# Two key pieces per output half, five shared relus, a later first y, and a mixed last-but-one tile

## Chip, cores and metric

One core of one Trainium2 chip. The metric is the device time of one execution in microseconds (us). The kernel before takes 1197.23 us (median of 3 runs, 1196.8 to 1197.61). Ratios further down are computed as the mean time of one kernel's runs over the mean of the other's runs of the same rounds, with a 95% interval; so they are not quite the ratio of the medians quoted beside them. A profiled execution has its own "span", which leaves out some 2 us of start and end.

## The reference

```python
def _attn_ref(u, v, z):                     # u, v: 8 x 3008 x 256; z: 8 x 3008 x 64
    scores = (1.0 / S) * np.matmul(z, z.transpose(0, 2, 1))
    attn = np.maximum(scores, 0.0) ** 2     # relu, then square
    return u * np.matmul(attn, v)

def _moe_ref(x, w_in, w_out):               # 24064 tokens, 256 -> 2048 -> 256
    h = x @ w_in
    return (h * np.cos(h)) @ w_out          # g = h cos(h); y = g w_out
```

The output is `_moe_ref` of `_attn_ref`, 24064 x 256 in fp32.

## The kernel before

The engines are named as in the profile: PE is TensorE (matmuls), ACT is ScalarE, DVE is VectorE, POOL is GpSimd, and SP issues the DMA of the turned pieces. SBUF is the working memory on the chip; PSUM is the memory that TensorE writes its sums to, divided into banks; a score group fills two of them, with 512 fp32 each in a partition. The 24064 tokens are 48 tiles, called columns while attention is computed for them: 8 batches of 6 columns, most of 512 tokens. For a column TensorE computes score groups (two key blocks of 128 keys each, against the column's 512 queries), ACT takes the relu out of PSUM, DVE squares it into a buffer A in SBUF, and TensorE multiplies A with v into two output halves, each gathered in two PSUM banks that are added at the end. The scores are symmetric, so many A pieces are not computed but turned (transposed) by DMA. A key piece is four key blocks of A, the unit in which the values are multiplied. There are three double banks E0, E1, E2 for scores, h and one output half, and two single banks M0, M1 for the other half and for y.

```python
    def emit_score(later=None):             # one score group
        ...
        e = E[take_e()]                     # a double bank: two halves of 512 fp32
        for t in range(2):
            nc.tensor.matmul(e[:, t, 0:Wt], zT[...], zT[...], ...)
        r = rpool.tile([P, 2, CW], FP16, name="r")
        nc.scalar.activation(r[:, :, 0:W], e[:, :, 0:W], AF.Relu)           # ACT
        def square():
            nc.vector.tensor_tensor(a4, r4, r4, ALU.mult)                   # DVE
        ...

    def gate_sum(s, b0, b1):                # the two banks of an output half, added
        sm = spool.tile([P, CW], FP32, name="sm")
        nc.scalar.copy(sm[:, 0:W], b0[:, 0:W])                              # ACT
        nc.vector.tensor_tensor(sm[:, 0:W], b1[:, 0:W], sm[:, 0:W], ALU.add)  # DVE
        return sm

    def phase_a_first(s, n, extra={}):      # columns 0, 1 and 2, one after the other
        pair = [E[ea][:, 0, :], E[ea][:, 1, :]]
        acc = [pair, M] if s == 1 else [M, pair]    # banks of output half 0 and half 1
        steps = [(dh, k) for I in range(NC) for dh in range(2)
                 for k in range(4 * I, min(4 * I + 4, last))] + [(2, last)]
        ...                                 # values, with the next column's scores between
        late_sums.extend(gate_sum(s, *acc[dh]) for dh in range(2))
        hold(late_sums[0][0:1, 0:1])        # POOL waits here, then loads u and (s = 1) w_out
        load_u(s + 1)
        e_order.append(ea)
```

The MoE stage s computes the h of tile s - 1 in 8 units (TensorE, into an E bank; ACT makes cos, DVE g) and the y of tile s - 2 between them. Stage 2 is the first one: it has the h of tiles 0 and 1, and the y of tile 0 between those. From tile 1 on, y is "mixed": Strassen-Winograd, seven products of half size in place of eight, with sums s1 on POOL and s2, s4 on DVE. The last two tiles (46, 47) are not mixed.

```python
    def mixed(m):
        return 1 <= m < NSLOT - 2           # NSLOT = 48
    order_y = (5, 1, 6, 7, 2, 3, 4)         # product 5 reads s1, 6 reads s2, 3 reads s4
    ...
        if n > 8:                           # stage 2, 16 h units: y block i stands behind
            after = (1, 3, 5, 7, 9, 11, 13, 14)     # h unit after[i], counted from 0
    ...
    phase_a_first(0, 12, {4: lambda: turn_late(4), 8: lambda: turn_late(5)})
    phase_a_first(1, 12)
    nc.gpsimd.dma_start(w_out16, moe_w_out.rearrange("(k p) f -> p k f", p=P))
    phase_a_first(2, 14)
```

Of the kernel before, what the change touches and what calls it, by code (L numbers as in the profile page):

```python
# [14 lines left out]
def kernel(  # L15
# [9 lines left out]
    nc = tc.nc  # L25
    AF = mybir.ActivationFunctionType
# [5 lines left out]
    P = 128  # L32
# [146 lines left out]
    turn_slots = {}  # L179
    done_groups = [0]  # L180

    def emit_score(later=None):
        b, J, I, h = groups[done_groups[0]]
        done_groups[0] += 1
        cut = I == J and not (b == 0 and J < 3)
        W = 2 * P if cut and h == 0 else width(J)
        zT = zTs[b]
        e = E[take_e()]
        for t in range(2):
            k = 4 * I + 2 * h + t  # L190
            half = t if h == 0 else 1 - t
            rows = slice(half * H, (half + 1) * H)
            Wt = min(W, (2 * h + t + 1) * P) if cut else W
            nc.tensor.matmul(  # L194
                e[:, t, 0:Wt],
                zT[rows, k * P:(k + 1) * P],
                zT[rows, J * CW:J * CW + Wt],
                start=True,
                stop=True,
            )  # L200
        key = (b, J, I)
        a = new_piece(key) if h == 0 else piece(key)
        r = rpool.tile([P, 2, CW], FP16, name="r")
        nc.scalar.activation(r[:, :, 0:W], e[:, :, 0:W], AF.Relu)  # L204
        def square():
            if I > J:
                a4 = a.rearrange("p (k t j) -> p t k j", k=4, j=P)[:, 2 * h:2 * h + 2, :, :]
                r4 = r.rearrange("p t (k j) -> p t k j", j=P)
                nc.vector.tensor_tensor(a4, r4, r4, ALU.mult)  # L209
            else:  # L210
                a4 = a.rearrange("p (k w) -> p k w", w=CW)[:, 2 * h:2 * h + 2, 0:W]
                nc.vector.tensor_tensor(a4, r[:, :, 0:W], r[:, :, 0:W], ALU.mult)  # L212

        if later is None:
            square()
        else:
            later.append(square)
        if h == 0:
            return
        if cut or (I > J and (b, J, I) not in direct):  # L220
            turns.append(((b, I), key))
            turns.sort(key=lambda t: t[0])
            turn_slots[key] = pieces[key]
            pending[pieces[key]] = "held"
# [122 lines left out]
    def phase_a_first(s, n, extra={}):  # L347
        b, J = s // NC, s % NC
        ea = e_order.pop(0)
        pair = [E[ea][:, 0, :], E[ea][:, 1, :]]  # L350
        acc = [pair, M] if s == 1 else [M, pair]
        last = NB - 1
        steps = [
            (dh, k)
            for I in range(NC)
            for dh in range(2)
            for k in range(4 * I, min(4 * I + 4, last))
        ] + [(2, last)]
        lo, hi = 5 if s == 0 else 2, 42
        at = {}  # L360
        for i in range(n):
            p = lo + (hi - lo) * i // (n - 1)
            at[p] = at.get(p, 0) + 1
        for i, (dh, k) in enumerate(steps):
            if i in extra:
                extra[i]()
            if dh == 2:
                emit_value(b, J, last, 0, 0, acc[0][0], False, True)
                emit_value(b, J, last, 1, 1, acc[1][1], False, True)
            else:  # L370
                for t in range(2):
                    emit_value(
                        b, J, k, t, dh, acc[dh][t], k == 0, k == last - 1 and t != dh
                    )
            if dh > 0 and (k % 4 == 3):
                drop_piece((b, J, k // 4))
                if s > 0:
                    emit_turns((0, 0), 1)
                    if k < 4:
                        turn_u(s)  # L380
                    elif k < 8:
                        for d in range(2):
                            gate_mul(s - 1, d, late_sums.pop(0))
            for _ in range(at.get(i, 0)):
                emit_score(later=squares if s == 0 and i == lo else None)
        if s == 0:
            turn_u(0)
        late_sums.extend(gate_sum(s, *acc[dh]) for dh in range(2))
        hold(late_sums[0][0:1, 0:1])
        load_u(s + 1)  # L390
        e_order.append(ea)
# [24 lines left out]
        )  # L416

    def mixed(m):
        return 1 <= m < NSLOT - 2

    F = NFT // 2
    T = 2 * P
# [38 lines left out]
            )  # L461
        nc.scalar.activation(y_outs[m][0][:, 1, :], acc, AF.Copy, bias=0.0, scale=inv_s2)

    def product(m, n):
        g = gs[m]
        nk, up, low = halves_of(m)
        nk = nk // P
        t = lambda i: w_mix[:, i, :, :]
        left, right = {
            1: (g[:, 0:F, up], w_out16[:, 0:F, 0:P]),  # L470
            2: (g[:, F:, up], w_out16[:, F:, 0:P]),
            3: (s4, w_out16[:, F:, P:D]),
            4: (g[:, F:, low], t(3)),
            5: (s1, t(0)),
            6: (s2, t(1)),
            7: (g[:, 0:F, low], t(2)),
        }[n]
        at = order_y.index(n) + (nk == 1 and n in order_y[4:])
        acc = M[at % 2][:, 0:nk * P]
        for ft in range(F):  # L480
            for k in range(nk):
                nc.tensor.matmul(  # L482
                    acc[:, k * P:(k + 1) * P],
                    left[:, ft, k * P:(k + 1) * P],
                    right[:, ft, :],
                    start=(ft == 0 and k == 0),
                    stop=(ft == F - 1 and k == nk - 1),
                )
        acc = acc.rearrange("p (k d) -> p k d", d=P)
        if n == 5:  # L490
            y_outs[m] = [opool.tile([P, 2, D], FP32, name="o") for i in range(2)]
            y_parts[m] = {}
        c11, c12, c21, c22 = (y_outs[m][i][:, 0:nk, d * P:(d + 1) * P] for i in range(2) for d in range(2))
        parts = y_parts[m]
        add = lambda dst, other: nc.vector.scalar_tensor_tensor(
            dst, acc, inv_s2, other, ALU.mult, ALU.add
        )
        if n in (1, 5, 6):
            parts[n] = ypool.tile([P, 2, P], FP32, name=f"p{n}")[:, 0:nk, :]
        if n in (1, 5):  # L500
            nc.scalar.activation(parts[n], acc, AF.Copy, bias=0.0, scale=inv_s2)
        elif n == 6:
            add(parts[6], parts[1])
            nc.gpsimd.tensor_tensor(c12, parts[6], parts[5], ALU.add)
        elif n == 7:
            add(c21, parts[6])
            nc.gpsimd.tensor_tensor(c22, c21, parts[5], ALU.add)
        elif n == 2:
            add(c11, parts[1])
        elif n == 3:  # L510
            add(c12, c12)
            store_half(m, 0, y_outs[m][0])
        else:
            add(c21, c21)
            store_half(m, 1, y_outs[m][1])

    def y_bank(m, k):
        if m == NSLOT - 1 and k == 3:
            return E[0][:, 0, 0:D]
        return M[k // 2][:, (k % 2) * D:(k % 2 + 1) * D]  # L520

    def y_block(m, ft, k):
        final = m == NSLOT - 1
# [58 lines left out]
    def phase_b(s):  # L582
        y, hs = s - 2, [(s - 1, i) for i in (0, 4, 1, 5, 2, 6, 3, 7)]
        if s == 2:
            hs = [(0, i) for i in range(8)] + hs
        for dh in range(len(late_sums)):
            gate_mul(s, 2 - len(late_sums), late_sums.pop(0), nc.gpsimd)
        if mixed(y):
            ys = [lambda n=n: product(y, n) for n in order_y]
            if mwidth(y) < CW:  # L590
                ys.insert(4, lambda: middle(y))
        else:
            ys = [lambda i=i: emit_y(y, i) for i in range(8)]
            ys[7] = lambda f=ys[7]: (f(), store_y(y))
        n = len(hs)
        if n > 8:
            after = (1, 3, 5, 7, 9, 11, 13, 14)
        elif mixed(y):
            after = (0, 1, 2, 3, 4, 5, 6, 6)
        else:  # L600
            after = (0, 1, 2, 3, 4, 5, 6, 6)
        for i, (m, unit) in enumerate(hs):
            times_c = emit_h(m, unit)
            if not mixed(y):
                times_c()
            for f, place in zip(ys, after):
                if place == i:
                    f()
            if mixed(y):
                times_c()  # L610
            if mixed(m) and unit >= 4:
                mix_early(m, unit - 4)
            if i in (1, 3, 5):
                emit_turns((0, 0), 1)
# [52 lines left out]
    emit_score(later=squares)  # L667
    emit_score(later=squares)
    turn_on_pe(2)
    copy_turned(2)  # L670
    squares.pop(0)()
    squares.pop(0)()
    M = [ppool.tile([P, CW], FP32, name=f"M{i}", tag=f"M{i}") for i in range(2)]

# [94 lines left out]
```

## Time and profile before

| | before |
|---|---|
| time, median | 1197.23 us |
| span of the profiled execution, clock | 1194.3 us, 1.0 |
| TensorE busy | 99% of the span |
| TensorE stands still near 24 us (column 0 to 1) | about 0.6 us |
| near 37 us (column 1 to 2) | 2.1 us |
| near 54 us (first y of the first MoE stage) | 1.7 us |
| anywhere behind that | never over 0.21 us |

How the lines are read: in the timeline a row has start, length, engine, source line, operation, tiles and shape, the number of instructions, and in brackets the idle time ahead and what ended it. A matmul's end is modelled; so a stop is best taken from start to start, against the usual pitch. The rows themselves are in the prediction.

### The profile page before, as it was taken

Reading aid. Unit: us, or ns where it says so; the run is one execution under the profiler, and the core shown is the slowest. Engines: PE = TensorE matmul, PEld = TensorE weight load, DVE = VectorE, ACT = ScalarE, POOL = GpSimd, SP = SyncE. Lnnn points to the kernel's source line nnn. Section 1 sums busy time; section 2 is a strip of 40 time slices with the busy share of each in tenths; the row PEclk is TensorE's granted clock in tenths of the full one; section 3 lists DMA queues with packets and bytes.
Section 4 is the critical chain, followed back from the end, with each engine's and each line's share of the span. In section 5 each row is a group of like instructions: output and inputs, shape, how many; then the busy total and the mean of one; then the engine's idle time right before and its main releaser. Section 6 shows DMA issues by size and latency. Waiting matters only on the chain.

```text
span 1194.3 us, 28924 instructions
## 1 busy us (share of the span) xinstructions
PE 1184.6 (99%) x11839; PEld 727.2 (61%) x11839; DVE 1008.6 (84%) x1293; ACT 795.1 (67%) x927; POOL 678.4 (57%) x707
## 2 busy tenths in 40 slices
PE   9899999999999999999999999999999999999998
PEld 4556655665566656566556665666656666665566
DVE  6798988888988898888988889888888888888775
ACT  7866666666766676666766676766766666666454
POOL 3186745557565573665647556476565765545450
PEclk9999999999999999999999999999999999999999
DMA  9999898769995699956999459974798838954301
GB/s 159 172 165 163 121 153 127 118 107 137 139 139 104 114 140 157 128 92 113 150 147 132 91 107 156 169 117 77 121 160 154 122 70 122 183 105 89 65 19 54
DMA packets 479861, 147.98 MB, mean 124 GB/s; under 512 B 404208, under 2 KB 479472, under 8 KB 479728
## 3 DMA queue, kind: packets, MB, share of 16 engines
q1 hardware_dynamic: 380752, 112.93, 54.5%
q0 software_dynamic: 97440, 32.78, 28.1%
q8 instruction: 92, 1.51, 0.5%
q10 hardware_dynamic: 1536, 0.43, 0.2%
q14 instruction: 41, 0.34, 0.1%
HBM read 66.32 MB, written 24.64 MB: 76 GB/s over the span
## 4 chain that ended last, share of the span: by engine, by line
PE 97%; ACT 1%; DVE 1%; issue 1%; ACTq 0%; DVEq 0%
PE E L403 27%; PE M L482 23%; PE M L258 20%; PE E L258 19%; PE E L194 5%; PE M L524 2%; ACT r L204 1%; PE M L459 1%; PE E L654 0%; DVE sm L270 0%; PE E L524 0%; DVE A L209 0%; DVE x L286 0%; DVE g L414 0%; PE M L677 0%
## 5 line engine op out<-in xcount | busy, mean ns | idle before, releaser
L411 ACT ACTIVATE c<-E 128x1024 f16<-128x1024 f32 (+1 forms) x384 | 385.6, 1006 | 218.0 <-PE E L403 214.8
L414 DVE SCALAR_TENSOR_TENSOR g<-E,c 128x1024 f16<-128x1024 f32 (+1 forms) x384 | 458.9, 1197 | 66.7 <-ACT c L411 65.7
L204 ACT ACTIVATE r<-E 128x512 f16<-128x512 f32 (+1 forms) x342 | 327.8, 967 | 114.1 <-PE E L194 108.4
L258 PEld LDWEIGHTS <-v 64*128 64x128 f16 x4512 | 246.8, 94 | 232.4 <-issue 20.6
L403 PE MATMUL E<-x,w_in 128*128 128x512 f16 (+1 forms) x1408 | 353.8, 375 | 0.0
L432 POOL TENSOR_TENSOR s<-g 128x512 f16<-128x512 f16 (+1 forms) x180 | 202.9, 1127 | 185.4 <-DVE g L414 138.9
L258 PE MATMUL M<-A,v 64*128 64x512 f16 (+1 forms) x2256 | 284.9, 372 | 2.1 <-ACT sm L269 1.2
L258 PE MATMUL E<-A,v 64*128 64x512 f16 (+1 forms) x2256 | 279.4, 372 | 0.0
L433 POOL TENSOR_TENSOR g<-g 128x512 f16<-128x512 f16 (+1 forms) x180 | 214.2, 1190 | 14.1
L403 PEld LDWEIGHTS <-w_in 128*128 128x128 f16 x1536 | 133.4, 98 | 108.6 <-issue 19.1
L482 PEld LDWEIGHTS <-g 128*128 128x128 f16 x2752 | 168.6, 98 | 39.8
L209 DVE TENSOR_TENSOR A<-r 128x1024 f16<-128x1024 f16 x240 | 173.3, 734 | 15.1 <-ACT r L204 14.3
L286 POOL TENSOR_TENSOR x<-sm,uT 128x512 f16<-128x512 f32 (+1 forms) x43 | 48.5, 1130 | 214.1 <-DVE sm L270 213.9
L482 PEld LDWEIGHTS <-s 128*128 128x128 f16 x2064 | 126.6, 98 | 30.6
L194 PE MATMUL E<-zT 64*128 64x512 f16 (+4 forms) x684 | 130.0, 356 | 0.5 <-ACT zT L647 0.3
L439 DVE TENSOR_TENSOR s<-s,g 128x1024 f16<-128x1024 f16 (+1 forms) x90 | 98.5, 1094 | 2.1 <-POOL s L432 2.1
L482 PE MATMUL M<-w_out,g 128*128 128x128 f16 x1376 | 91.5, 219 | 0.0
L482 PE MATMUL M<-w_mix,g 128*128 128x128 f16 x1376 | 91.5, 219 | 0.0
L482 PE MATMUL M<-w_mix,s 128*128 128x128 f16 x1376 | 91.5, 219 | 0.0
L212 DVE TENSOR_TENSOR A<-r 128x512 f16<-128x512 f16 (+1 forms) x102 | 80.7, 792 | 10.2 <-ACT r L204 9.4
L194 PEld LDWEIGHTS <-zT 64*128 64x128 f16 x684 | 39.3, 94 | 36.7 <-issue 2.2
L441 DVE TENSOR_TENSOR s<-g,s 128x1024 f16<-128x1024 f16 (+1 forms) x90 | 59.4, 662 | 0.0
(58 smaller groups left out, 657.6 us busy)
## 6 DMA issues: line engine op xcount, KB each, us to landing
out_dram<-o SPq DMA_DIRECT2D x87, 256.0 KB, 2.2
v<-in_v_dram POOLq DMA_DIRECT2D x40, 256.0 KB, 9.2
u<-in_u_dram POOLq DMA_DIRECT2D x40, 256.0 KB, 4.8
A<-A SPq DMA_TRANSPOSE x252, 5.2
z<-in_z_dram POOLq DMA_DIRECT2D x14, 192.0 KB, 10.6
z<-in_z_dram POOLq DMA_DIRECT2D x14, 176.0 KB, 6.3
v<-in_v_dram POOLq DMA_DIRECT2D x8, 192.0 KB, 12.0
u<-in_u_dram POOLq DMA_DIRECT2D x8, 192.0 KB, 4.0
```

The costliest lines, as they stand in the source:

```text
L194: nc.tensor.matmul(e[:, t, 0:Wt], zT[rows, k * P:(k + 1) * P], zT[rows, J * CW:J * CW + Wt], start=True, stop=True,)
L204: nc.scalar.activation(r[:, :, 0:W], e[:, :, 0:W], AF.Relu)
L209: nc.vector.tensor_tensor(a4, r4, r4, ALU.mult)
L212: nc.vector.tensor_tensor(a4, r[:, :, 0:W], r[:, :, 0:W], ALU.mult)
L258: nc.tensor.matmul(bank[:, 0:width(J)], vs[b, k // 4][t * H:(t + 1) * H, k % 4, dh * P:(dh + 1) * P], value_rhs(b, J, k, t), start=start, ...
L403: nc.tensor.matmul(e[:, f, 0:W], w_in16[:, k, ft * P:(ft + 1) * P], x[:, k, 0:W], start=(k == 0), stop=(k == 1),)
L411: nc.scalar.activation(c[:, :, 0:W], e[:, :, 0:W], AF.Sin, bias=half_pi, scale=inv_s2)
L414: return lambda: nc.vector.scalar_tensor_tensor(gs[m][:, 2 * i:2 * i + 2, 0:W], e[:, :, 0:W], 1.0, c[:, :, 0:W], ALU.mult, ALU.mult)
L432: nc.gpsimd.tensor_tensor(s1[:, f, 0:n], g[:, f, low], g[:, lower, low], ALU.add)
L433: nc.gpsimd.tensor_tensor(g[:, f, low], g[:, f, up], g[:, f, low], ALU.subtract)
L439: nc.vector.tensor_tensor(s2[:, f, 0:n], s1[:, f, 0:n], g[:, f, up], ALU.subtract)
L482: nc.tensor.matmul(acc[:, k * P:(k + 1) * P], left[:, ft, k * P:(k + 1) * P], right[:, ft, :], start=(ft == 0 and k == 0), stop=(ft == F - ...
```

## The change

The intent, as its words say: relieve ACT at the ends of the first columns (five relus shared with DVE), use the M banks later in columns 1 and 2 (two key pieces, that is eight key blocks, per output half), put the first y of stage 2 behind the third h unit, and take one matmul product in eight out of tile 46. The numbers in `shared_groups` count the score groups from 0, as the prediction does; the tables further down count them from 1. The diff, cut to its core:

```diff
+    shared_groups = {0, 14, 15, 26, 27}
 ...
-        nc.scalar.activation(r[:, :, 0:W], e[:, :, 0:W], AF.Relu)
+        n = 1 if shared else 2
+        nc.scalar.activation(r[:, 0:n, 0:W], e[:, 0:n, 0:W], AF.Relu)
+        if shared:
+            nc.vector.tensor_scalar(r[:, 1, 0:W], e[:, 1, 0:W], 0.0, None, ALU.max)
 ...
+            parts = [slice(0, 1), slice(1, 2)] if done == 0 else [slice(0, 2)]
+            for t in parts:
+                nc.vector.tensor_tensor(a4[:, t], r4[:, t], r4[:, t], ALU.mult)
 ...
+        run = 1 if s == 0 else 2
         steps = [
-            for I in range(NC)
+            for I in range(0, NC, run)
             for dh in range(2)
-            for k in range(4 * I, min(4 * I + 4, last))
+            for k in range(4 * I, min(4 * (I + run), last))
 ...
-        return 1 <= m < NSLOT - 2
+        return 1 <= m < NSLOT - 1
 ...
+        bank = 1 - k // 2 if m == NSLOT - 1 else k // 2          # y banks of the last tile
 ...
+                for i, n in enumerate((1, 5) + order_y[2:] if late else order_y)   # late: s == NSLOT
 ...
-            after = (1, 3, 5, 7, 9, 11, 13, 14)
+            after = (2, 4, 6, 7, 9, 11, 13, 14)
+        elif s == NSLOT:
+            after = (0, 1, 3, 4, 5, 6, 7)
 ...
+            if s == NSLOT and i in (1, 3):
+                for c in range(2):
+                    mix_late(y, "s2" if i == 1 else "s4", c)
 ...                                       # first group: its square ahead of a copy
+    squares.pop(0)()
     copy_turned(2)
-    squares.pop(0)()
```

More of the change, by code (lines that the diff above doesn't have):

```diff
@@ L180 @@
     done_groups = [0]
+    shared_groups = {0, 14, 15, 26, 27}
     def emit_score(later=None):
-        b, J, I, h = groups[done_groups[0]]
+        done = done_groups[0]
+        b, J, I, h = groups[done]
         done_groups[0] += 1
@@ L203, in emit_score @@
         r = rpool.tile([P, 2, CW], FP16, name="r")
-        nc.scalar.activation(r[:, :, 0:W], e[:, :, 0:W], AF.Relu)
+        shared = done in shared_groups
+        n = 1 if shared else 2
+        nc.scalar.activation(r[:, 0:n, 0:W], e[:, 0:n, 0:W], AF.Relu)
+        if shared:
+            nc.vector.tensor_scalar(r[:, 1, 0:W], e[:, 1, 0:W], 0.0, None, ALU.max)
         def square():
@@ L208, in square @@
                 r4 = r.rearrange("p t (k j) -> p t k j", j=P)
-                nc.vector.tensor_tensor(a4, r4, r4, ALU.mult)
             else:
                 a4 = a.rearrange("p (k w) -> p k w", w=CW)[:, 2 * h:2 * h + 2, 0:W]
-                nc.vector.tensor_tensor(a4, r[:, :, 0:W], r[:, :, 0:W], ALU.mult)
+                r4 = r[:, :, 0:W]
+            parts = [slice(0, 1), slice(1, 2)] if done == 0 else [slice(0, 2)]
+            for t in parts:
+                nc.vector.tensor_tensor(a4[:, t], r4[:, t], r4[:, t], ALU.mult)
         if later is None:
@@ L462, in middle, with product @@
         nc.scalar.activation(y_outs[m][0][:, 1, :], acc, AF.Copy, bias=0.0, scale=inv_s2)
-    def product(m, n):
+    def product(m, n, place):
         g = gs[m]
@@ L477, in product @@
         }[n]
-        at = order_y.index(n) + (nk == 1 and n in order_y[4:])
-        acc = M[at % 2][:, 0:nk * P]
+        acc = M[(place + (nk == 1 and place >= 4)) % 2][:, 0:nk * P]
         for ft in range(F):
@@ L489, in product @@
         acc = acc.rearrange("p (k d) -> p k d", d=P)
-        if n == 5:
+        if m not in y_outs:
             y_outs[m] = [opool.tile([P, 2, D], FP32, name="o") for i in range(2)]
@@ L519, in y_bank @@
             return E[0][:, 0, 0:D]
-        return M[k // 2][:, (k % 2) * D:(k % 2 + 1) * D]
+        bank = 1 - k // 2 if m == NSLOT - 1 else k // 2
+        return M[bank][:, (k % 2) * D:(k % 2 + 1) * D]
     def y_block(m, ft, k):
@@ L588, in phase_b @@
         if mixed(y):
-            ys = [lambda n=n: product(y, n) for n in order_y]
+            late = s == NSLOT
+            ys = [
+                lambda n=n, i=i: product(y, n, i)
+                for i, n in enumerate((1, 5) + order_y[2:] if late else order_y)
+            ]
             if mwidth(y) < CW:
```

## The prediction

> **What bounds the kernel now.** I read the page first, then the chain of waits, then the timeline of the first 80 us and of the last 80, and last the groups kept apart by form, for durations. From the page:
>
> ```profile
> PE 1184.6 (99%) x11839; PEld 727.2 (61%) x11839; DVE 1008.6 (84%) x1293; ACT 795.1 (67%) x927; POOL 678.4 (57%) x707
> PE 97%; ACT 1%; DVE 1%; issue 1%; ACTq 0%; DVEq 0%
> ```
>
> TensorE is busy 99% of the span and owns 97% of the chain that ended last. So the time is the sum of TensorE's work and of its few stalls; another engine matters only where TensorE stands still for it. The timeline shows where that is, all of it in the first columns and the MoE stage after them (figures: start us, length us; in brackets the idle time before and what ended it):
>
> ```profile
> 24.47 0.59 PE L258 MATMUL M<-A,v 64*128 64x512 f16 x3 [0.28 <-DVE sm L270]
> ...
> 37.69 0.37 PE L258 MATMUL M<-A,v 64*128 64x512 f16 x1 [1.22 <-ACT sm L269]
> 38.65 0.80 PE L258 MATMUL M<-A,v 64*128 64x512 f16 x5 [0.59 <-DVE sm L270]
> ...
> 55.52 1.05 PE L524 MATMUL M<-w_out,g 128*128 128x256 f16 x8 [1.58 <-DVE g L414]
> ```
>
> The idle times count from a matmul's modelled end; by starts, against a pitch of 0.216 us for a pair of half-height matmuls of 512 columns, the stops are about 0.6 us in all near 24, 2.1 us near 37 (column 1 to column 2: the M banks wait for ACT's copy and DVE's addition) and 1.7 us near 54 (the first y waits for the first g). From there to the end there is no stop over 0.2 us.
>
> **What the Trainium skill says.**
> - "TensorE: Matmul & The Clock Gate", the section on why 56 and not 53.3 ns: warm matmuls start N/2.4 GHz plus about 2.5 ns apart, 55.6 ns for 128 columns, 215.7 for 512. The trace agrees: four matmuls of 512 columns of an h unit take 0.86 us of start-to-start time.
> - "VectorE: DVE Perf Modes", the perf-mode tier table with its note on PSUM operands: fp32 out of PSUM goes at one element a cycle. The trace agrees: the addition `sm` with 512 fp32 elements from PSUM takes 0.68, while the copy of 512 fp16 elements from PSUM takes 0.42. So the new relu half on DVE (512 fp32 from PSUM) is estimated at 0.69 us.
> - "GPSIMD Engine Reference", specifications: GpSimd shares SBUF interfaces with VectorE, and they contend on two-input DVE work. The trace shows `s` (two fp16 inputs) at 0.68 us alone and at 1.64 in one case beside POOL. It matters at the end of the changed kernel.
>
> The durations I use, from the groups by form (busy us, mean ns):
>
> ```profile
> L204 ACT ACTIVATE r<-E 128x1024 f16<-128x1024 f32 x289 | 293.6, 1025 | 92.1 <-PE E L194 86.4 <-DVE A L209 1.1
> L204 ACT ACTIVATE r<-E 128x512 f16<-128x512 f32 x45 | 27.1, 602 | 14.6 <-PE E L194 14.6
> L270 DVE TENSOR_TENSOR sm<-M,sm 128x512 f32<-128x512 f32 x40 | 27.2, 681 | 1.3 <-ACT sm L269 1.3
> ```
>
> **The change part by part.** The order of instructions, built for both kernels, differs only in the first columns, the MoE stage behind them and the last stage; between them it is the same.
>
> *Shared relus (groups 0, 14, 15, 26, 27).* ACT does one half (0.60 instead of 1.02), DVE the other. The built program makes DVE's half wait for ACT's half of the same group, so the halves go one after the other: 0.60 + 0.69 = 1.3 us until the score bank is free, against 1.02; and DVE gets 0.6 us more (0.69 less the 0.08 by which neighbours overlap) per group just where its additions are awaited. The end of column 1 before:
>
> ```profile
> 36.70 0.69 DVE L212 TENSOR_TENSOR A<-r 128x1024 f16<-128x1024 f16 x1 [0.38 <-ACT r L204]
> 37.05 0.59 ACT L269 COPY sm<-M 128x512 f32<-128x512 f32 x1
> 37.31 0.68 DVE L270 TENSOR_TENSOR sm<-E,sm 128x512 f32<-128x512 f32 x1
> 37.91 0.68 DVE L270 TENSOR_TENSOR sm<-M,sm 128x512 f32<-128x512 f32 x1
> ```
>
> M1 is free at 38.59. After, on the same clock: square 25 ends 35.30, DVE's half of 26 runs 35.22 to 35.91, square 26 to 36.63, half 27 to 37.24, square 27 to 37.96, addition E to 38.56, addition M to 39.16. ACT's copies cannot start sooner, since they wait for the last matmul at 36.5. Cost: 39.16 − 38.59 = +0.57 us.
>
> *Column 0 to column 1.* Before, M's first use after four key blocks meets the addition (24.42), and the second score of column 1 meets the addition of E (25.02), so TensorE passes that score at 25.07. With two key pieces per half, M is used later and that wait goes; but the score bank's wait stays behind it. After: half 14 on DVE ends 22.49, square 14 at 23.21, half 15 at 23.82 (the first score of column 1 wants that bank at 23.37 and waits 0.5), square 15 at 24.54, addition M at 25.14, addition E at 25.74. The second score passes at 25.79 instead of 25.07: +0.72 us. So by this walk the two-piece order gains nothing itself here, and the shared relus cost.
>
> *The first group.* DVE's half, the split square and the later turned copy fall in a stretch in which TensorE runs fillers and waits for z; the score that waits for the bank goes from 7.40 to 7.49, the next from 8.10 to about 8.1. I take 0.
>
> *The MoE stage.* Before: h, h, then y 0, which waits for g: ends at 54.24 (addition of E) plus 1.22. After, a third h stands between. It needs the E bank of the addition: it starts at 54.29 (0.5 of a stop after h 2 would have ended at 53.78), runs to 55.15, and y 0 starts at 55.52 (0.37 of a stop). Stops 0.5 + 0.37 = 0.87 instead of 1.74: −0.87 us. The g rate is enough behind it (1.14 us apart against 1.3 for TensorE).
>
> *The last stage.* y of tile 46 becomes seven products instead of eight blocks. A unit now (from the timeline):
>
> ```profile
> 1115.26 1.03 PE L403 MATMUL E<-x,w_in 128*128 128x512 f16 x4
> 1116.12 1.06 PE L482 MATMUL M<-w_mix,g 128*128 128x128 f16 x16
> 1117.01 1.03 PE L403 MATMUL E<-x,w_in 128*128 128x512 f16 x4
> ...
> 1172.40 1.03 PE L403 MATMUL E<-xodd,w_in 128*128 128x512 f16 x4
> 1173.26 1.04 PE L524 MATMUL M<-w_out,g 128*128 128x256 f16 x8
> 1174.13 1.03 PE L403 MATMUL E<-xodd,w_in 128*128 128x512 f16 x4
> ```
>
> A product takes 1117.01 − 1116.12 = 0.89, a block 0.87: 8 × 0.87 − 7 × 0.89 = 0.73 us less work. But there is no attention phase between mixing and products here. The last s1 sum on POOL can start when the last g of tile 46 ends (1171.40) and takes 1.16: product 5 reaches it at 1172.21 and waits till 1172.70. The second s2 half on DVE follows g 1 (about 1174.08), two times 0.6: ready at 1175.24, and product 6 ends at 1175.74 instead of the ideal 1175.04. So 0.7 of the 0.73 goes into a stop. I take −0.05 us.
>
> Sum: 0.72 + 0.57 − 0.87 − 0.05 = +0.37 us, that is 1197.6.
>
> **The rivals.**
> 1. The change gains what it was written for. If the DVE half ran in less time than 0.69, or the halves overlapped, the additions would come as early as before or 0.1 us earlier; with the MoE stage and a part of the end, 1195.8 to 1196.4. For it: whoever chose five such groups likely timed them. Against it: the wait in the program, and the 0.68 of the like-sized additions.
> 2. The end loses more: if POOL is late, or its work and DVE's s2, s4 collide (the 1.64 us case), products wait a further 0.5 to 1 us, and the eight g, four mixes and five sums keep DVE full to the last y: 1198 to 1198.6. Against it: POOL's last pair should be over at 1173.9, as the s2 work starts.
> 3. The mixing of a tile more loads POOL (8 operations of 1.16 us) in the stage before; hidden, as the like stages show POOL idle 0.8 us before its last sum. Nothing.
>
> **Range and chances.** My walk gives 1197.6; rival 1 draws down and rival 2 up less. I put 1197.4, with 1196.2 to 1198.6 as the range. 2% would be 24 us; all the stops together are under 5 us, so within 2% is as good as certain.
>
> **What would show it.** In the changed profile: DVE's relu halves near 0.69 us, each starting after ACT's half; score stops of about 0.5 and 1.0 us near 24 and 25; the M stop near 37 grown to about 2.7; the stop before the first y down to under 0.5, with one of 0.5 before the third h; the last y starting at about 1183.2 (1182.82 before, plus the sum of 0.37). It is wrong if the halves overlap, if the stop near 37 shrinks, or if products 5 and 6 do not wait.

## The result, and the profile after

The changed kernel takes 1197.57 us (median of 4 runs, 1196.39 to 1198.71), the one before 1197.01 us in runs of the same kind (median of 4, 1196.61 to 1197.61). The ratio is 1.0004, with a 95% interval of 0.9987 to 1.0021: the same within what can be told, and the predicted 1197.4 is inside the noise. That the median comes within 0.2 us of the 1197.4 is luck: the four times lie in two pairs 2 us apart (1196.39, 1196.69 and 1198.44, 1198.71), and the profile, which is one of the lower pair, is what tells the parts. From its page:

```profile
PE 1183.7 (99%) x11887; PEld 726.6 (61%) x11887; DVE 1013.9 (85%) x1308; ACT 793.0 (66%) x927; POOL 688.9 (58%) x717
PE 96%; DVE 2%; ACT 1%; issue 1%; DMA 0%; POOL 0%; ACTq 0%; DVEq 0%
```

TensorE has 0.9 us less work than before (1184.6), and the span is still 0.6 us longer (1194.9 against 1194.3): more standing still, and DVE's share of the chain is 2% for 1%. The timeline of TensorE, at the places that answer to those shown of before:

```profile
24.09 0.39 PE L197 MATMUL E<-zT 64*128 64x512 f16 x2 [0.31 <-DVE r L211]
...
26.02 0.39 PE L197 MATMUL E<-zT 64*128 64x512 f16 x2 [0.89 <-DVE sm L280]
...
38.63 0.37 PE L268 MATMUL M<-A,v 64*128 64x512 f16 x1 [1.22 <-ACT sm L279]
40.14 0.80 PE L268 MATMUL M<-A,v 64*128 64x512 f16 x5 [1.14 <-DVE sm L280]
...
55.79 1.02 PE L414 MATMUL E<-x,w_in 128*128 128x512 f16 x4 [0.34 <-DVE sm L280]
57.02 1.05 PE L535 MATMUL M<-w_out,g 128*128 128x256 f16 x8 [0.21 <-DVE g L425]
...
1173.34 0.40 PE L492 MATMUL M<-w_mix,s 128*128 128x128 f16 x4 [0.32 <-POOL s L443]
```

Every one of the announced waits is there, most in the announced size (start to start 0.47 and 1.05 near 24 us for 0.5 and 1.0 said, 2.67 near 38 for 2.7, 0.51 and 0.37 near 56 for 0.5 and less than 0.5): a score of column 1 for DVE's relu half, the next score for the second addition, M1 for the addition between columns 1 and 2, the third h for the addition, the first y for g (now short), and product 5 for POOL's last sum. Why the additions are late is to be read on DVE, at the ends of column 0 and column 1, together with the group of the relu halves:

```profile
L211 DVE TENSOR_SCALAR r<-E 128x512 f16<-128x512 f32 x5 | 3.4, 684 | 0.8 <-ACT r L209 0.8
```

```profile
22.03 0.69 DVE L211 TENSOR_SCALAR r<-E 128x512 f16<-128x512 f32 x1
...
24.07 0.69 DVE L222 TENSOR_TENSOR A<-r 128x1024 f16<-128x1024 f16 x1
24.68 0.68 DVE L280 TENSOR_TENSOR sm<-M,sm 128x512 f32<-128x512 f32 x1
25.28 0.68 DVE L280 TENSOR_TENSOR sm<-E,sm 128x512 f32<-128x512 f32 x1
...
38.81 0.68 DVE L280 TENSOR_TENSOR sm<-E,sm 128x512 f32<-128x512 f32 x1
39.41 0.68 DVE L280 TENSOR_TENSOR sm<-M,sm 128x512 f32<-128x512 f32 x1
```

From 22.03 to the end of the addition of E at 25.96 DVE has six instructions behind one another (two relu halves, two squares, two additions) with under 0.1 us between them; the kernel before had four there. The last addition ends at 40.09, where before it ended at 38.59; of these 1.50 us, 0.95 were carried over from what came before group 18, and 0.55 are new.

For the sums I cut the span at TensorE starts that both kernels have: the 1st, 15th, 18th and 29th score group of all, the first score behind the first MoE stage ("stage 3" in the next table), and the last y.

| stretch (TensorE, start to start) | before | after | difference | predicted |
|---|---|---|---|---|
| start to score group 1 | 5.46 | 5.43 | -0.03 | 0 |
| group 1 to 15 (column 0) | 15.10 | 15.36 | +0.26 | 0 |
| group 15 to 18 (column 0 to 1) | 4.51 | 5.23 | +0.72 | +0.72 |
| group 18 to 29 (column 1 to 2) | 14.02 | 14.57 | +0.55 | +0.57 |
| group 29 to the first score behind stage 2 | 37.13 | 36.27 | -0.86 | -0.87 |
| from there to the last y | 1106.60 | 1106.54 | -0.06 | -0.05 |
| last y to the end of the span | 11.51 | 11.51 | 0 | 0 |
| span | 1194.33 | 1194.91 | +0.58 | +0.37 |

### The profile page after: what moved, and what is told of

Same layout as the page of the kernel before. It is cut to its first block, busy times and chain, and to the rows that moved or that the text cites. A ratio compares the mean times of both kernels' runs of the same rounds, so it can differ in the third digit from the quotient of the medians.

```text
span 1194.9 us, 29048 instructions
## 1 busy us (share of the span) xinstructions
PE 1183.7 (99%) x11887; PEld 726.6 (61%) x11887; DVE 1013.9 (85%) x1308; ACT 793.0 (66%) x927; POOL 688.9 (58%) x717
## 4 chain that ended last, share of the span: by engine, by line
PE 96%; DVE 2%; ACT 1%; issue 1%; DMA 0%; POOL 0%; ACTq 0%; DVEq 0%
PE E L414 27%; PE M L492 23%; PE M L268 20%; PE E L268 19%; PE E L197 5%; PE M L535 1%; ACT r L209 1%; DVE A L222 1%; PE M L470 1%; DVE sm L280 0%; DVE r L211 0%; DMA z<-in_z_dram 0%; DVE g L425 0%; PE E L535 0%; DVE x L296 0%
## 5 line engine op out<-in xcount | busy, mean ns | idle before, releaser
L443 POOL TENSOR_TENSOR s<-g 128x512 f16<-128x512 f16 (+1 forms) x184 | 207.6, 1128 | 189.5 <-DVE g L425 139.9
L222 DVE TENSOR_TENSOR A<-r 128x1024 f16<-128x1024 f16 (+2 forms) x343 | 251.8, 745 | 24.2 <-ACT r L209 22.5
L444 POOL TENSOR_TENSOR g<-g 128x512 f16<-128x512 f16 (+1 forms) x184 | 218.9, 1190 | 14.4
L492 PEld LDWEIGHTS <-g 128*128 128x128 f16 x2816 | 172.5, 98 | 40.8
L492 PEld LDWEIGHTS <-s 128*128 128x128 f16 x2112 | 129.4, 98 | 32.1 <-DVE s L450 0.5
L492 PE MATMUL M<-w_mix,s 128*128 128x128 f16 x1408 | 94.0, 219 | 0.3 <-POOL s L443 0.3
L279 ACT COPY sm<-E 128x512 f32<-128x512 f32 (+1 forms) x48 | 27.7, 577 | 42.7 <-PE E L268 42.7
```

Source lines behind the costliest of these rows:

```text
L222: nc.vector.tensor_tensor(a4[:, t], r4[:, t], r4[:, t], ALU.mult)
L443: nc.gpsimd.tensor_tensor(s1[:, f, 0:n], g[:, f, low], g[:, lower, low], ALU.add)
L444: nc.gpsimd.tensor_tensor(g[:, f, low], g[:, f, up], g[:, f, low], ALU.subtract)
L492: nc.tensor.matmul(acc[:, k * P:(k + 1) * P], left[:, ft, k * P:(k + 1) * P], right[:, ft, :], start=(ft == 0 and k == 0), stop=(ft == F - ...
```

## The experiments

Twelve kernels ran, most as five timed rounds beside the kernel before (a profiled execution is among the times). The same cuts, for all of them, in us:

| kernel | to group 1 | 1 to 15 | 15 to 18 | 18 to 29 | 29 to stage 3 | to last y | rest | span |
|---|---|---|---|---|---|---|---|---|
| before | 5.46 | 15.10 | 4.51 | 14.02 | 37.13 | 1106.60 | 11.51 | 1194.3 |
| changed | 5.43 | 15.36 | 5.23 | 14.57 | 36.27 | 1106.54 | 11.51 | 1194.9 |
| e1_no_share | 5.71 | 15.10 | 4.51 | 14.02 | 36.27 | 1106.55 | 11.51 | 1193.7 |
| e2_share_only | 5.50 | 15.55 | 5.22 | 14.58 | 39.29 | 1106.60 | 11.52 | 1198.3 |
| e3_act_halves | 5.50 | 14.95 | 4.57 | 14.38 | 37.55 | 1106.55 | 11.51 | 1195.0 |
| e4_moe_only | 5.36 | 14.88 | 4.51 | 14.21 | 37.66 | 1106.60 | 11.52 | 1194.7 |
| e6_end_order | 5.68 | 15.30 | 4.51 | 14.03 | 37.12 | 1106.02 | 12.01 | 1194.7 |
| e7_swap | 5.61 | 15.10 | 3.91 | 13.43 | 40.97 | 1106.55 | 11.51 | 1197.1 |
| e11_best_fill | 5.51 | 15.67 | 3.91 | 13.42 | 36.98 | 1106.01 | 11.52 | 1193.0 |
| e12_after_fill | 5.58 | 15.20 | 5.22 | 14.57 | 36.27 | 1106.55 | 11.50 | 1194.9 |
| e13_swap_split | 5.71 | 15.04 | 3.91 | 13.43 | 40.90 | 1106.01 | 11.74 | 1196.7 |
| e14_swap_early | 5.37 | 15.10 | 3.91 | 13.42 | 36.37 | 1106.01 | 11.70 | 1191.9 |
| e15_kept_split | 5.68 | 15.24 | 4.51 | 14.02 | 37.07 | 1106.02 | 11.76 | 1194.3 |
| e16_one_piece | 5.50 | 15.10 | 4.75 | 13.61 | 36.27 | 1106.01 | 11.50 | 1192.7 |

Two things are seen at once. The third, fourth and sixth figure repeat to 0.02 us where nothing in them was changed (except the fourth in e3 and e4, 14.38 and 14.21, where a slow stretch begins, of which more below), so a profile tells parts that the timed runs can't. And the first two move by up to 0.6 us between kernels whose first 20 us are the same (e11 and e14, say): in e11 TensorE waits 0.63 us for a cast of z on POOL, in e14 it does not; that is the start of the execution, not the part under test.

### Sharing undone (e1), sharing alone (e2)

```diff
-    shared_groups = {0, 14, 15, 26, 27}      # e1: the changed kernel, less this part
+    shared_groups = set()                    # (square whole, turned copy first again)
```

e2 is the opposite: the changed kernel with `run = 1`, the old `after`, and tile 46 not mixed, so that sharing alone is left.

> The changed kernel with the shared relus taken out (ACT does both halves of every relu again, one square per group, the turned copy back ahead of the first square); the two-piece order, the MoE order and the last stage stay. Theory A (DVE's chain of relu halves and squares delays the two additions at the ends of columns 0 and 1): the score stops near 24 and 25 fall from 0.47 + 1.05 to about 0.6 in all, the M stop near 38 falls from 1.29 to 0.74, and the 0.23 lost before 22 us comes back; the profiled span is 1193.4, against 1194.9 for the changed kernel and 1194.3 for the one before, and the time over the kernel before is 0.9992. Theory B (the stops come from the two-piece order, and the shared relus shorten them): the stops stay or grow, span 1194.9 to 1195.5.

> The kernel before with the shared relus alone. Theory A: all of the start's loss is there without the two-piece order: the first score of column 1 after the stops passes 0.95 later (0.23 at the start, 0.72 at the column's end), the first score of column 2 1.50 later, and nothing is won back: span 1195.8, ratio 1.0013. Theory B: no loss without the two-piece order: span 1194.3 or less, ratio 0.9995 to 1.0.

e1: 1195.70 us (median of 5, 1195.03 to 1196.67) against 1197.48 (9 runs), ratio 0.9989 (0.9977 to 1.0002). e2: 1199.15 us (1197.23 to 1200.06), ratio 1.0010 (0.9996 to 1.0024). In the table e1 has the 4.51 and 14.02 of the kernel before, e2 the 5.22 and 14.58 of the changed one. So all of the +0.72 and +0.55 is the shared relus, whether the two-piece order is there or not. TensorE in e1, at the two ends of columns:

```profile
25.32 0.39 PE L197 MATMUL E<-zT 64*128 64x512 f16 x2 [0.66 <-DVE sm L280]
...
38.90 0.80 PE L268 MATMUL M<-A,v 64*128 64x512 f16 x5 [0.58 <-DVE sm L280]
```

The score's wait for DVE's second addition is alone there now, with 0.82 from start to start (about 0.6 was expected); the M wait at 24 is gone by the two-piece order, as the walk had it, and nothing is gained by that. What comes back in column 0 (0.26 expected) can't be told from the sums: 15.10 in e1 and before, but 14.88 to 15.67 in other kernels without sharing, 15.20 to 15.55 in the three with it. One wait speaks for a part of it: in the changed kernel the first value matmuls wait for DVE's first square,

```profile
9.41 0.61 PE L268 MATMUL M<-A,v 64*128 64x512 f16 x4 [0.28 <-DVE A L222]
```

a stop of 0.44 from start to start. e2 has one of 0.50 at the same place, and no kernel without sharing has it; but e12, which shares too, has none.

e2 missed its span (1198.3 for 1195.8) in the first MoE stage, 39.29 for 37.13, with a wait that no theory had:

```profile
57.77 1.03 PE L535 MATMUL M<-w_out,g 128*128 128x256 f16 x8 [2.06 <-DMA w_out<-in_moe_w_out_dram]
```

The load of w_out is issued by POOL behind the additions at the end of column 1 (at 41.07 here), and it took 16.6 us to land. Later additions make a later load; here it ran past g. But the stop, 2.22 us from start to start, is only 0.48 longer than before (1.74). The other 1.7 us (an estimate: 2.16 less 0.48) are lost behind it, where the granted clock is 0.86 from 56 to 60 us and 0.71 from 60 to 64: the slow stretch that e4 below shows.

### Which part of sharing costs (e3)

```diff
-            nc.vector.tensor_scalar(r[:, 1, 0:W], e[:, 1, 0:W], 0.0, None, ALU.max)
+            nc.scalar.activation(r[:, 1, 0:W], e[:, 1, 0:W], AF.Relu)
```

> The changed kernel with the second relu half of the five groups as a second ACT instruction: the relu is still in two steps, one after the other, but DVE has none of it. It parts the two reasons of theory A. If DVE's added 0.6 us a group is the cost, the additions come as early as in the run without sharing, and the span is 1193.4 to 1193.7. If the cost is that a score bank is held for two steps instead of one (1.1 to 1.3 us against 1.02), the stops stay near those of the changed kernel: span 1194.6 to 1195.

1196.79 us (1195.41 to 1197.69), ratio 0.9995 (0.9982 to 1.0007). The stretch from group 15 to 18 is 4.57 and M1's stop between columns 1 and 2 is 0.74 again, as in e1:

```profile
25.02 0.39 PE L197 MATMUL E<-zT 64*128 64x512 f16 x2 [0.72 <-DVE sm L280]
```

So a relu in two steps is nearly free (0.06), and DVE's 0.6 us more per group is the cost. The span of 1195.0 is by itself the number of the other theory (1194.6 to 1195). It holds a stretch of slow matmuls (next part): from group 18 to stage 3 e3 takes 51.93 us and e1 50.29. Without these 1.64 it would be about 1193.3 (an estimate), near the 1193.4 to 1193.7 of the first theory.

A relu half on DVE that lies beside ACT's half, and not behind it, was not run. By the author's account, giving it a tile of its own left the wait in the built program, which treats the two halves of a score bank as one tile. The Trainium skill ("PSUM — Partial Sum Buffer", on bank collisions) says that ScalarE and VectorE may work on different banks at the same time; the halves are in two banks of 512 fp32 each, so the wait would not be one of the chip. No run here shows it. At the ends of columns it would have won little: there ACT's half was over (at 21.88, 22.90, 36.12 and 37.19) before DVE came to its own (22.03, 23.36, 36.16 and 37.48), and only in the first group did DVE stand idle for it, 0.80 us. A fused relu and square in one DVE instruction was refused by the language, since both inputs would be in PSUM (again without a run).

### The later first y alone (e4), and the slow stretch (e12)

```diff
-            after = (1, 3, 5, 7, 9, 11, 13, 14)      # e4: the kernel before
+            after = (2, 4, 6, 7, 9, 11, 13, 14)
```

> The kernel before with the later first y of the third MoE stage alone (first y behind the third h unit). My step: the stop of 1.74 before the first y becomes 0.5 before the third h and 0.37 before the first y, 0.86 less, and it is kept to the end: span 1193.4, ratio 0.9993. Rival: what is won comes back as a stop later in that stage (g too slow for the y blocks, or the drained banks), and the span stays 1194.3.

1195.53 us (1195.08 to 1197.0), ratio 0.9989 (0.9977 to 1.0002). The two stops are the predicted ones:

```profile
55.55 1.02 PE L414 MATMUL E<-x,w_in 128*128 128x512 f16 x4 [0.34 <-DVE sm L280]
56.79 1.05 PE L535 MATMUL M<-w_out,g 128*128 128x256 f16 x8 [0.21 <-DVE g L425]
```

From start to start they are 0.51 and 0.37 against 1.74. But the profiled span, 1194.7, is longer than that of the kernel before, and the times fall into two groups. The reason stands in the windows view (columns: window, us, busy times of PE, PEld, DVE, ACT and POOL, granted clock, DMA share, GB/s):

```profile
34.00:38.00 4.00, 2.52 (x21) 1.09 (x18) 3.06 (x6) 3.27 (x5) 0.18 (x1) 1.00 1.19 198
38.00:42.00 4.00, 3.67 (x20) 1.62 (x21) 0.96 (x2) 1.29 (x2) 1.90 (x2) 0.57 0.96 148
```

Right behind the 2.1 us in which TensorE stands still between columns 1 and 2, the granted clock is 0.57 for 4 us: matmul pairs of 512 columns start 0.43 us apart for 3 us, and not 0.216. Group 18 to stage 3 takes 51.87 us here and 50.29 in e1, so the slow stretch costs 1.6 us. e3 has the same stretch at the same place; e2, e7 and e13, with stops of 2.2 us and more near 55, have one behind those. The profiles of the kernel before, the changed one, e1, e2 and e6 have a stop of 2.1 us or more near 37 too, and no slow stretch behind it: what decides whether it comes is not known. Of the 44 executions of the kernel before, 18 took 1195.9 to 1196.7 us, 24 took 1197.3 to 1198.8, and two lay between. Where the mean clock is on record (40 of them), it is 1.0 in 15 of 17 short ones and 0.998 or 0.999 in 22 of 23 long ones. So the two groups are likely the executions without and with a slow stretch; no long execution of this kernel was profiled.

e12 is the changed kernel with ten dummy matmuls on zeroed data into the free score bank, in that stop:

```diff
     phase_a_first(1, 12)
+    for i in range(10):
+        nc.tensor.matmul(E[e_order[0]][:, 0, :], warm[:, 0:P], warm, start=True, stop=True)
```

> The changed kernel, with ten dummy matmuls (2.15 us) on TensorE between columns 1 and 2, where it stands still for 2.67 us in two pieces. Some executions of every kernel so far are 1.3 to 2 us longer at a granted clock of 0.998 or 0.999, and two of their profiles show a stretch of half-speed matmuls for some 3 us right behind that stop. Theory: the stop itself makes the clock drop. Then, with TensorE kept busy, no profile and no timed run shows the slow stretch there, the five times are within 0.5 us of each other near 1196.5, and the clock is 1.0. Rival (the clock drops for another reason, or anywhere): times still fall in two groups, 1196.5 and 1198.5, or the dummies cost their time.

1196.60 us, and the five times are 1196.43, 1196.51, 1196.60, 1196.68 and 1197.22, while 7 of the 11 runs of the kernel before beside it took over 1197.4. The dummies cost nothing (14.57 from group 18 to 29, as without them), and the clock is whole in its profile:

```profile
38.00:42.00 4.00, 3.85 (x27) 1.69 (x27) 2.04 (x4) 1.38 (x3) 2.07 (x3) 1.00 1.11 198
```

So the runs speak for the stop as what makes the slow stretch possible: five of five executions without it are short, where 20 of 44 of the kernel before are (by chance about 2%, an estimate from these counts), and all five slow stretches in the profiles follow on a stop of 2.1 us or more. They do not show what else decides it. Two parts of the expectation were missed: the five times lie 0.79 apart and not within 0.5, and the mean clock was 1.0 in three of the five and 0.999 in two. In the profile, one of the two, the missing 0.001 is not a slow stretch: the clock is 0.69 from 1192.0 to 1194.3, behind the last matmul.

### The end (e6)

```diff
-                for i, n in enumerate((1, 5) + order_y[2:] if late else order_y)
+                for i, n in enumerate((1, 2, 5, 6, 7, 3, 4) if late else order_y)
```

on the kernel before with nothing of the change but the mixed tile 46.

> The kernel before with the last stage of the change alone (seven products for tile 46) and its products in another order: 1, 2, 5, 6, 7, 3, 4 in place of 1, 5, 6, 7, 2, 3, 4. Product 2 needs no sum, so products 5 and 6 come one place later. My step (the stops at products 5 and 6, 0.48 and 0.14 us in the changed kernel, come from POOL's and DVE's sums and eat the 0.73 that the seventh product saves): both stops go, the last y starts about 0.7 earlier after the last stage's scores than in the kernel before (1106.60 us after the first score of slot 3 there, 1106.54 in the changed kernel, 1105.9 here), span 1193.6. Rival (the end is bound by g and DVE's load, whatever the order): the stops move to products 3, 4 or the last y, and the start of the last y is within 0.1 of the changed kernel's.

1196.45 us (1195.61 to 1197.33), ratio 0.9993 (0.998 to 1.0006). The stretch to the last y is 1106.02 against 1106.60 before and 1106.54 in the changed kernel, and products 5 and 6 no longer wait:

```profile
1174.59 1.06 PE L492 MATMUL M<-w_mix,s 128*128 128x128 f16 x16
...
1176.35 1.06 PE L492 MATMUL M<-w_mix,s 128*128 128x128 f16 x16
...
1182.66 5.40 PE L535 MATMUL M<-w_out,g 128*128 128x256 f16 x48
```

So 0.52 of the 0.63 us that the change leaves in those two stops is to be had by the order alone; a small stop of 0.1 at 1180.9 is new. The span missed 1193.6 by what comes ahead of group 15 (0.4) and 0.5 us behind the last matmul, where the output lands; e11 and e16 have the same end without that 0.5.

### The additions turned round (e7)

```diff
-        late_sums.extend(gate_sum(s, *acc[dh]) for dh in range(2))
+        second = gate_sum(s, *acc[1])
+        late_sums.extend([gate_sum(s, *acc[0]), second])
```

on e1. In column 0 this adds the E pair first, in column 1 the M pair, in column 2 the E pair.

> The changed kernel without shared relus, and with the order of the two additions at the end of columns 0, 1 and 2 turned round: first the pair that the next column does not begin with is left to wait, and the one it needs first is added first. My theory (the last of DVE's two additions sets each stop): near 24 the stop before the second score falls from 0.82 to 0.2, near 37 M1 comes free 0.6 earlier, and the MoE stage's two stops stay 0.9 in sum, as g follows both additions: from the first score of column 0 to the first score of slot 3 it is 68.7 us against 69.9 in the run without sharing, span 1192.5. Rival (ACT's copies or the squares set the stops): less than 0.3 is gained in sum.

Both stops shrink by the predicted 0.6: group 15 to 18 is 3.91, 18 to 29 13.43. Yet the median is 1196.75 us (1193.97 to 1200.32), the ratio 0.9996 (0.9981 to 1.0011), and the profile shows why, on DVE:

```profile
54.03 1.29 DVE L222 TENSOR_TENSOR A<-r 128x1024 f16<-128x1024 f16 x2 [3.88 <-DMA A<-A]
```

A square waited 3.88 us for the DMA that turns an A piece, whose buffer it overwrites. That transpose, and the like one in e1 and in e14 (below), where w_out is loaded earlier, took from issue to landing (last figure, us):

```profile
A<-A SPq DMA_TRANSPOSE x1, 15.0
...
A<-A SPq DMA_TRANSPOSE x1, 8.5
...
A<-A SPq DMA_TRANSPOSE x1, 6.0
```

In e7 it was issued at 38.95 and landed at 53.94, while the 1 MB of w_out was under way (issue to landing 17.6 us; 14.6 in e1). The 9.25 us that a later expectation names is another thing: how long SP's instruction that issues the next transpose took. The Trainium skill ("DMA: Bandwidth & Descriptors", "Issuing engines are not separate DMA queues") says that transfers started by different engines run on the same 16 DMA engines and interleave, and this agrees with it. The first MoE stage takes 40.97 us where it takes 36.27 in e1: about 3.2 of the 4.7 are stops (3.24 and 0.87 us, for 0.51 and 0.37), the rest, about 1.5, a slow stretch behind them. So what the change in order wins (1.2 us) is in part lost, in some executions and not in others, and the expected span of 1192.5 came as 1197.1.

### Together (e11, e13, e14, e15)

e11 is e7 with the order of products of e6 and four of the dummies of e12:

```diff
-                for i, n in enumerate((1, 5) + order_y[2:] if late else order_y)
+                for i, n in enumerate((1, 2, 5, 6, 7, 3, 4) if late else order_y)
     phase_a_first(1, 12)
+    for i in range(4):
+        nc.tensor.matmul(E[e_order[0]][:, 0, :], warm[:, 0:P], warm, start=True, stop=True)
```

> All that the runs so far favour: no shared relus, two-piece order, additions turned round, first y behind the third h, seven products at the end in the better order, and four dummy matmuls (0.86 us) on TensorE into a free score bank between columns 1 and 2, in a stop that is longer than they are. If the parts add up: span 1191.9 and ratio about 0.9975 to the kernel before. If stops only trade places: span over 1192.8.

1195.41 us (1193.98 to 1200.3), ratio 0.9992 (0.9976 to 1.0007); span 1193.0 for 1191.9, which by its own mark (over 1192.8) is the number of the other reading. The parts add up but at the start, where TensorE waits for z (15.67 for 15.10), and at the first y (36.98 for 36.27):

```profile
55.67 1.03 PE L536 MATMUL M<-w_out,g 128*128 128x256 f16 x8 [1.44 <-DMA w_out<-in_moe_w_out_dram]
```

So w_out was the next thing to move. e13 splits its load, as below; e14 also puts the two halves ahead of `phase_a_first(1, 12)`, which is behind the additions of column 0; both have five dummies. e15 is e13 without the turned additions, and with eight dummies.

```diff
-    nc.gpsimd.dma_start(w_out16, moe_w_out.rearrange("(k p) f -> p k f", p=P))
+    w_out_rows = moe_w_out.rearrange("(k p) f -> p k f", p=P)
+    for f in range(0, NFT, NFT // 2):
+        nc.gpsimd.dma_start(w_out16[:, f:f + NFT // 2, :], w_out_rows[:, f:f + NFT // 2, :])
```

> The kernel of all favoured parts (no shared relus, turned additions, better order at the end, five dummies between columns 1 and 2), with the load of w_out in two halves: the first y needs the first half only. In that kernel's profile the first y waited 1.60 us for this load, which landed 15.5 us after its issue at 40.0. Theory (the load of w_out is what took the gain back in the third MoE stage): the first y starts 53.7 to 54.5 instead of 55.67, span 1191.3 to 1192, and no run is over 1196. Rival (the DMA queue as a whole is too slow there, the transposes as well, one of which took 9.25 us beside the load in one profile): some runs still have 1196 to 1200, by stops before a square that waits for a transpose.

> The same, with both halves of w_out loaded from the end of column 0 (issue near 26.5) and not from the end of column 1 (near 39.5). Between 28 and 32 us the DMA engines moved 78 GB/s, between 42 and 54 they moved 158 to 185. If the load's place is what hurts, the transposes of column 2 take 2 to 5 us each in place of 5 to 9, the first y waits for g alone, span 1191.3 to 1192 in all runs. Rival: the load then delays the transposes of column 1, the squares or values of column 1 or 2 wait for them, and the span is over 1193.

> The careful version: the changed kernel without shared relus, with the additions in their old order, the better order of products at the end, eight dummies (1.72 us) in the stop of 2.1 us between columns 1 and 2, and w_out in two halves. From the run without sharing (1193.7): less 0.6 at the end, the dummies hidden: span 1193.1, every timed run at clock 1.0 and within 1194.3 to 1195.2, ratio 0.998. Rival: the runs still fall into groups over 1 us apart.

e13: 1193.61 us; four of its six times are 1193.27 to 1193.81, two are 1196.98 and 1198.52. Its profile fell in a bad one, with a square that waits 3.83 us for a transpose (the like one as in e7, here 14.8 us). This fits the rival, the DMA as a whole; splitting is not enough. e14: 1194.49 us (1193.46 to 1194.64, and one of 1196.59), ratio 0.9981 (0.9969 to 0.9994), span 1191.9 as expected. No transpose holds up a square in its profile, and the first y waits for g alone:

```profile
36.89 1.26 PE L268 MATMUL M<-A,v 64*128 64x512 f16 x6
...
54.33 1.05 PE L536 MATMUL M<-w_out,g 128*128 128x256 f16 x8 [0.71 <-DVE g L426]
```

(The first line is behind the dummies, with only 0.24 of a stop left there.) "In all runs" was too much: the five spans are 1191.9, 1192.9, 1192.7, 1194.8 and 1191.7, three of them above 1192. e15: 1194.74 us (1194.49 to 1196.08), ratio 0.9984 (0.9972 to 0.9996), span 1194.3 for 1193.1; a square waited 1.45 us for a transpose here too, and two of the five times (1195.39, 1196.08) lie above the expected 1195.2.

### What two key pieces are worth (e16)

```diff
-        run = 1 if s == 0 else 2       # e14, with the old order of columns 1 and 2
+        run = 1
```

> The kernel with the turned additions and the early load, with columns 1 and 2 in the old order (one key piece per output half). What is the two-piece order worth? By the walk on record nothing in the changed kernel, since the score bank's wait stands behind the one that it removes. Turned additions change that: column 1 in the old order needs M after four key blocks, and M is now added second (at 25.0 and not at 24.4). Theory: from the eighth score pair before the end of column 0 to the score behind the stops (20.47 to 24.38, 3.91 us, with two pieces) it takes 5.0 here, so the two-piece order is worth 1.1 at the end of column 0, where both orders had 4.51 before; between columns 1 and 2 nothing changes (13.42). Span 1193. Rival: the two-piece order is worth nothing here either: 3.91 again, span 1191.9.

1194.53 us (1194.51 to 1195.38, the five within 0.9 us of one another), ratio 0.9983 (0.997 to 0.9997), span 1192.7. Group 15 to 18 is 4.75 where e14 has 3.91: M is needed early, and waits for the addition that is now second:

```profile
25.11 0.59 PE L268 MATMUL M<-A,v 64*128 64x512 f16 x3 [0.59 <-DVE sm L280]
```

So the two-piece order, worth nothing in the change as it stands, is worth 0.84 us in the profile once the additions are turned round (1.1 were expected), and 0.19 between columns 1 and 2 (0 expected). In the timed runs the two kernels, of different calls, can't be told apart.

Of all versions e13, e14, e15 and e16 beat the kernel before, which ran beside them, clear of the interval, at 0.9981 to 0.9984; none by 2%.

## Why the prediction was right

- *Column 0 to 1, +0.72, and column 1 to 2, +0.57*: measured +0.72 and +0.55. Both are the shared relus (e1, e2), and in them DVE's part (e3). The estimated 0.69 us for a half was 0.684. The prediction also says that the score bank is held 0.60 + 0.69 us, one after the other; at the ends of columns that was not what counted, since ACT's half was over before DVE reached its own: DVE's own row of instructions made it late.
- *The MoE stage, -0.87*: measured -0.86, by the two stops named, 0.51 and 0.37; e4 alone has the same two. The last y came at 1183.40, where 1183.2 was said.
- *The last stage, -0.05*: measured -0.06. Products 5 and 6 wait 0.48 and 0.14; without these waits the stretch is 0.52 shorter (e6). One line was misread beside it: sums of 1.64 us beside POOL are not "one case", since 39 of the 82 s2 sums of the kernel before (128x1024) took over 1.5. Nothing came of it, as the two last ones of the changed kernel took 1.28 together.
- *The first group, 0*: the profile has +0.26, and the runs do not settle it. The scatter of this stretch between like kernels is as large; but the stop of 0.44 for DVE's first square, which e2 has too, is one that the walk did not have, so part of it is likely the sharing, and the 0 is doubtful.
- *The sum, +0.37*: +0.58 in the profile. The blend to 1197.4 drew the figure the wrong way, by 0.2; nothing spoke for the rival that drew it there (the halves do not overlap, none of the two stops shrank).
- *Rival 2* (the end loses more) did not come: no product waits more than 0.48, and the last y starts without a stop.
- What the prediction did not have: two groups of times 1.3 to 2 us apart. The noise that hides the change is likely the slow stretch behind the stop near 37 us, and the load of w_out, which a later addition pushes towards the first y (it landed 0.25 us ahead of the first y already before, 55.27 for 55.52). The prediction counted that stop as its own 2 us alone.

## What to carry to other kernels

A step taken off one engine and given to another costs where the other's work is the one waited for: before sharing, read which engine ends the wait, not which one is busy. Of two things that both hold the next stage up, the order in which they are done can be worth more than making one quicker; and a reordering that wins nothing may be what makes another one possible. When TensorE must wait a microsecond or two, dummy matmuls can be worth their place (here they cost nothing), and when an earlier start is won, look at once for the transfer that it now meets.

## What the Trainium skill lacked or had wrong

- "TensorE: Matmul & The Clock Gate", Part 1 and "HAM oscillation": its rule is to leave TensorE no idle gaps over about 3.4 us. Here 2.1 us of standing still in two pieces (1.38 and 0.74), with a few matmuls around them, were enough in two (e3, e4) of seven profiles with such a stop or a somewhat longer one: in e4 the clock was 0.57 over 4 us behind it, and 1.6 us were lost; 24 of 44 executions of the kernel before lie in the longer group of times. With dummy matmuls in the stop, five of five executions stayed under 1197.3. What else decides it is open. The page's doubled pitch agrees (0.43 us a pair for 0.216).
- "DMA: Bandwidth & Descriptors": no page has how much a DMA transpose in SBUF is slowed by an ordinary load beside it. Here a transpose of a 128x2048 fp16 piece took 8.5 us from issue to landing in one execution and 15.0 in another of nearly the same program, both beside the 1 MB load of w_out, and 6.0 where that load came earlier (one profile each).
- "PSUM — Partial Sum Buffer" lets ScalarE and VectorE read different banks together; no page says that a program may still make them wait for each other when both banks are one tile, as here: in the first group DVE stood idle 0.80 us, until ACT's half (5.87 to 6.46) was over, and began at 6.50.
